# The end of an attention + soft-MoE kernel: PSUM bank order, filler matmuls, and a second queue for stores

**Chip, cores and metric.** One core of one Trainium2 chip. The metric is the device time of one execution in microseconds (us). Times from a trace are counted from the start of its span.

## The reference

The attention takes q, k, v of 8 x 12 x 448 x 64 in f32, with a soft cap on the scores. Its output, 3584 rows of 768, goes through a soft mixture of experts with 32 slots.

```python
def _attn_ref(q, k, v, cap):
    scores = scale * np.matmul(q, k.transpose(0, 1, 3, 2))
    scores = cap * np.tanh(scores / cap)
    ... softmax over the keys ...
    return np.matmul(attn, v)

def _moe_ref(x, phi, w1, w2):          # x: 3584 x 768, 8 experts, 4 slots each, F = 1024
    logits = x @ phi
    d = softmax(logits, axis=0)        # dispatch: over the rows
    slot_input = (d.T @ x)             # 32 x 768
    slot_out = relu(slot_input[e] @ w1[e]) @ w2[e]     # for each expert e
    c = softmax(logits, axis=1)        # combine: over the slots
    return c @ slot_out                # 3584 x 768, f32: 11 MB to store
```

The result is 11.0 MB. A softmax over all rows stands between the attention and the experts, so no row can be stored before the last row of attention is done.

## The kernel before

The kernel is scheduled by hand: the order of calls is the order of instructions on each engine. A tile framework adds the waits. It gives out the banks of PSUM (the memory into which TensorE writes) and the semaphores (counters) on which the completion of a DMA is counted. There are three places to know.

The attention's end. The pools of scores (`sc`, two tiles of three banks) and of `pv` (one bank) are closed, and a pool of seven banks takes their place. Its tiles `pvm` and `pvl` hold the last two pairs of heads, and `junk` is the target of filler matmuls. A filler is a 128x128 matmul of ones whose result nobody reads.

```python
    exp_part(NCH - 1, 0, CL)
    exp_part(NCH - 1, CL, CH)
    attp.close()
    big = mid.enter_context(tc.tile_pool(name="big", bufs=7, space=PSUM, reuse_waits="tile"))
    ...
    pvm = [bank([P, 2, VW], name=f"pvm{half}") for half in range(2)]
    junk = bank([P, P], name="junk")
    pv2 = [bank([P, 2, VW], name=f"pvl{half}") for half in range(2)]
    x_transp(last - 2)
    for half in range(2):
        pv_tiles(last - 1, half, 0, NT, pvm[half])
        norm(last - 1, half)
    logits(NQ - 2, bank([P, NG, NS], name="lpl"))
    busy(6)
    ...
```

The reloads of w2. The second layer's weights that don't fit in SBUF during attention lie in DRAM as bf16 and are read back, 384 KB at a time, by SyncE's queue (SP), first the first column halves, then the second. The last of them, `w2t60` of half 1, is used by the last four matmuls of the second layer.

```python
    for half in range(2):
        for n0 in range(R2, len(blocks), 4):
            t = tl.tile([P, 4, HD], BF16, name=f"w2t{n0}_{half}")
            sp.dma_start(out=t, in_=w2d[(n0 - R2) // 4][:, half, :, :])
            w2t[n0, half] = t
```

The stores. The output goes out as 24 half tiles of 192 KB (`obh`) and then 16 whole tiles of 384 KB (`ob`). VectorE (DVE) and ScalarE (ACT) take turns in moving a tile out of PSUM. The first ten half tiles are computed between the matmuls of the second layer's second half. All stores are issued by SP.

```python
    for n0 in range(0, n2, 4):
        layer2(n0, 1)
        if n0 >= 4 and n0 % 8 == 4 and done < NH - 2:
            for eng in ("act", "dve"):
                half_tile(done, 0, bank([P, HD], name="op0"), eng)   # matmul, evict, store
                done += 1
```

The softmax here doesn't subtract the row's maximum and nothing guards it: scores larger than these inputs give would overflow.

## Time and profile before

| | kernel before |
|---|---|
| device time, median of the first 3 runs | 326.57 us (326.3 to 327.66) |
| span of the profiled run | 325.5 us (this run: 327.26) |
| last tanh ends, last norm of the attention starts | 271.63, 277.33 |
| last reload issued | 281.8 |
| first store issued | 292.42 |
| DMA engines full from | 295.4 |
| 99% of the stored bytes moved, last byte landed | 323.2, 324.0 |

ScalarE limits the first 270 us (tanh and exp). After that one short step waits for another until the stores begin. Then the DMA engines are full, and the end comes when the bytes are out. So there are two ways to gain: start the stores earlier, or move more bytes in the first us of the store stage. The prediction shows the lines of the chain and of the windows. One more view is needed, SP's own timeline (start, duration of the group, line, what, count):

```profile
279.90 2.51 SPq L565 DMA_DIRECT2D w2t<-w2d  x5
292.42 7.80 SPq L624 DMA_DIRECT2D out_dram<-obh  x13
```

Five reloads are issued by 282.4, and then nothing until the first store at 292.42: the reloads are long issued when the stores begin.

### The profile page before, as it was taken

The numbers are of one execution on the slowest core, as the hardware profiler recorded it, in microseconds if no ns is written. First come the engines' busy times: TensorE is split into PE (matmuls) and PEld (weight loads), VectorE is DVE, ScalarE is ACT, GpSimd is POOL, SyncE is SP. The second block draws the span as 40 slices with busy tenths as digits, with TensorE's granted clock in tenths as the row PEclk, the third lists the DMA queues.
The fourth block names the chain that finished last, engine by engine and source line by source line (L and its number), as shares of the span: only waits on it lengthen the run. The fifth ranks groups of instructions, "written<-read, shape, count | busy, mean of one in ns | idle before, by whom it ended". The sixth has DMA issues, their size and how long they took to land.

```text
span 325.5 us, 8742 instructions
## 1 busy us (share of the span) xinstructions
PE 275.4 (85%) x3776; PEld 193.0 (59%) x3776; DVE 168.8 (52%) x428; ACT 283.5 (87%) x205; POOL 104.6 (32%) x133
## 2 busy tenths in 40 slices
PE   7889998889889988998889888988898877998570
PEld 6556666666666766666566666756666657642220
DVE  3535664466447653665466546644565343327442
ACT  2998999999999999999999999999999996226450
POOL 2064524533443353345334524452443020200000
PEclk9999999999999999999999999999999997999855
DMA  8689999999999989999999999999999435757997
GB/s 256 203 172 238 211 274 236 219 237 252 241 202 247 253 190 228 259 265 224 207 250 251 233 200 238 264 248 192 231 258 210 125 96 196 255 233 286 373 397 302
DMA packets 58486, 76.89 MB, mean 236 GB/s; under 512 B 3920, under 2 KB 54096, under 8 KB 58448
## 3 DMA queue, kind: packets, MB, share of 16 engines
q0 software_dynamic: 30480, 25.22, 51.1%
q1 hardware_dynamic: 27680, 50.67, 46.1%
q8 instruction: 29, 0.48, 0.6%
q10 hardware_dynamic: 288, 0.46, 0.4%
q14 instruction: 9, 0.07, 0.1%
HBM read 90.54 MB, written 18.09 MB: 334 GB/s over the span
## 4 chain that ended last, share of the span: by engine, by line
ACT 78%; PE 11%; DMA 3%; DVE 3%; issue 2%; SPq 1%; DVEq 0%; ACTq 0%
ACT ex L253 39%; ACT ex L257 38%; PE so_ps L609 2%; PE hp L583 2%; DMA out_dram<-ob 1%; PE op L635 1%; SPq L624 1%; DMA kraw<-in_k_dram 1%; PE junk L455 1%; PE sc L246 1%; PE pvm L274 1%; PE op L678 1%; DVE ob L682 1%; DMA out_dram<-obh 1%; PE pvl L274 1%
## 5 line engine op out<-in xcount | busy, mean ns | idle before, releaser
L253 ACT ACTIVATE ex<-sc 128x1344 bf16<-128x1344 f32 x112 | 161.6, 1712 | 2.7 <-PE sc L246 1.4
L257 ACT ACTIVATE ex<-ex 128x2688 bf16<-128x2688 bf16 (+2 forms) x57 | 160.2, 2831 | 0.1
L274 PEld LDWEIGHTS <-ex 128*128 128x128 bf16 x1344 | 79.6, 98 | 22.9 <-DVE xq L285 14.3
L274 PE MATMUL pv<-vbd,ex 128*128 128x130 bf16 x1288 | 90.4, 220 | 2.6 <-ACT ex L257 1.5
L246 PE MATMUL sc<-qT,kT 64*64 64x448 bf16 x672 | 78.8, 358 | 12.6 <-ACT ex L253 11.3
L224 POOL CAST vbd<-vraw 64x896 bf16<-64x896 f32 x23 | 21.4, 929 | 106.0 <-PE pv L274 81.3
L284 DVE RECIPROCAL rec<-pv 128x4 f32<-128x4 f32 x92 | 16.8, 183 | 60.1 <-PE pv L274 60.1
L246 PEld LDWEIGHTS <-kT 64*64 64x64 bf16 x672 | 28.3, 105 | 29.4 <-issue 11.7
L285 DVE TENSOR_TENSOR xq<-pv,rec 128x256 bf16<-128x256 f32 x92 | 39.1, 425 | 3.2
L455 PEld LDWEIGHTS <-ones 128*128 128x128 bf16 x446 | 27.7, 102 | 12.0 <-DVE xq L285 8.6
L328 POOL COPY e<-E 128x512 bf16<-128x512 bf16 x9 | 5.5, 610 | 88.4 <-ACT E L322 50.3
L455 PE MATMUL junk<-ones 128*128 128x128 bf16 x413 | 30.7, 221 | 3.0 <-DVE xq L285 1.9
L216 DVE COPY kT<-kps 128x896 bf16<-128x896 bf16 x23 | 14.4, 625 | 29.4 <-PE kps L214 29.4
L105 POOL DMA_DIRECT2D w1b<-in_moe_w_dram x32 | 24.9, 781 | 0.0
L225 POOL CAST vbd<-vraw 64x896 bf16<-64x896 f32 x23 | 24.0, 1042 | 1.3
L302 DVE COPY xT<-xps 128x512 bf16<-128x512 bf16 x47 | 19.5, 415 | 2.1 <-PE xps L300 2.1
L300 PE MATMUL xps<-ident,xq 128*128 128x128 bf16 x188 | 18.3, 220 | 0.7 <-DVE zacc L339 0.7
L203 DVE CAST kbf<-kraw 128x896 bf16<-128x896 f32 x22 | 17.2, 780 | 0.0
L216 DVE COPY qT<-qps 128x896 bf16<-128x896 bf16 x23 | 14.2, 618 | 4.5 <-PE qps L214 4.5
L214 PE MATMUL kps<-ident,kbf 128*128 128x128 bf16 x161 | 12.8, 219 | 4.2 <-DVE slacc L374 2.2
L214 PE MATMUL qps<-ident,qbf 128*128 128x128 bf16 x161 | 12.8, 219 | 3.2 <-DVE lg L316 2.7
L214 PEld LDWEIGHTS <-kbf 128*128 128x128 bf16 x161 | 10.0, 97 | 9.0 <-issue 8.3
(100 smaller groups left out, 232.5 us busy)
## 6 DMA issues: line engine op xcount, KB each, us to landing
w1b<-in_moe_w_dram POOLq DMA_DIRECT2D x32, 384.0 KB, 8.7
vraw<-in_v_dram SPq DMA_DIRECT2D x23, 448.0 KB, 4.6
qraw<-in_q_dram SPq DMA_DIRECT2D x22, 448.0 KB, 7.6
kraw<-in_k_dram SPq DMA_DIRECT2D x22, 448.0 KB, 5.2
w2d<-in_moe_w_dram POOLq DMA_DIRECT2D x18, 384.0 KB, 9.3
w2t<-w2d SPq DMA_DIRECT2D x18, 384.0 KB, 5.5
out_dram<-ob SPq DMA_DIRECT2D x16, 384.0 KB, 3.9
w2b<-in_moe_w_dram POOLq DMA_DIRECT2D x14, 384.0 KB, 9.0
```

Of the source, the lines that this page charges most:

```text
L105: pool.dma_start(out=w1b[e][:, js, fs], in_=w1r[:, e, js, fs])
L214: pe.transpose(ps[:, c, :], src[:, c, :], ident)
L216: dve.tensor_copy(t, ps)
L224: pool.tensor_copy(t[0:HP, :, :, 0:DH], raw[0:HP])
L225: pool.tensor_copy(t[HP:P, :, :, DH + 1:VW - 1], raw[HP:P])
L246: pe.matmul(sc[cs, u, 0:S], qkT["k", Q][r, c, cs], qkT["q", Q][r, :, cs], start=True, stop=True)
L253: act.activation(exs[j][:, half * CS:half * CS + CS, :], scores.pop(i)[:, :, 0:S], ACT.Tanh, scale=qk_scale / cap)
L257: act.activation(exs[j][:, u0:u1, :], exs[j][:, u0:u1, :], ACT.Exp, scale=cap)
L274: pe.matmul(pvs[pr, half][:, n, 0:VW], exs[j][:, u, GOFF[g]:GOFF[g] + P], vbds[Q % 2][:, h, c, :], start=(c == 0 and n == 0), stop=(c == N ...
L285: dve.tensor_tensor(xq[Q][:, 2 * half:2 * half + 2, h * P:(h + 1) * P] .rearrange("p g (i d) -> p g i d", i=2), pv[:, :, :, 0:DH], rec.to_ ...
L302: dve.tensor_copy(t, ps)
L455: pe.matmul(junk if home is None else home, ones, ones, start=True, stop=True)
```

## The change

The intent is threefold. One: ask for the banks at the attention's end in the order in which they come free, so that `pvm` need not wait for the last tanh. Two: add fillers in the last two steps, so that TensorE keeps its full clock. Three: issue the stores of ScalarE's tiles on ScalarE's own DMA queue, so that SP need not order all of them.

```diff
+    for j, slot, n in ((NCH - 2, "c", 6), (NCH - 2, "d", 10), (NCH - 1, "a", 8), (NCH - 1, "d", 10)):
+        at(j, slot, spare, n)
...
+    pv2 = [bank([P, 2, VW], name=f"pvl{half}") for half in range(2)]
+    lp2 = bank([P, NG, NS], name="lpl")
     pvm = [bank([P, 2, VW], name=f"pvm{half}") for half in range(2)]
     junk = bank([P, P], name="junk")
-    pv2 = [bank([P, 2, VW], name=f"pvl{half}") for half in range(2)]
...
-    logits(NQ - 2, bank([P, NG, NS], name="lpl"))
-    busy(6)
+    logits(NQ - 2, lp2)
+    busy(10)
...
-    def store(n, h0, h1, src):
+    def store(n, h0, h1, src, eng):
-        sp.dma_start(out=bass.AP(tensor=out.tensor,
+        eng.dma_start(out=bass.AP(tensor=out.tensor,
...
-        store(n, half, half + 1, ob)
+        store(n, half, half + 1, ob, act if eng == "act" else sp)
...
-        store(n, 0, 2, obs[n].rearrange("p a d -> p (a d)"))
+        store(n, 0, 2, obs[n].rearrange("p a d -> p (a d)"), sp if n % 2 else act)
```

## The prediction

> **What bounds the kernel now.** I read the page first (shares, slices, chain), then the chain of waits in order of time, then windows over the end. For the first 270 us ScalarE is the limit: the page's slices give ACT 9 tenths nearly throughout, and the chain spends 78% of the span in tanh and exp. None of the three parts touches that work, so the question is only what stands after the last tanh, at 271.6 us of a 325.5 us span. The chain of waits there (start, duration, what):
>
> ```profile
> 269.26 2.37 ACT ex L253 x2
> 271.63 0.05 issue
> 271.68 2.27 PE pvm L274 x28
> 273.95 0.21 PE lpl L311 x8
> 274.16 0.64 PE junk L455 x6
> 274.80 0.43 PE xps L300 x4
> 275.23 1.66 PE pvl L274 x20
> 276.89 0.17 PE junk L455 x3
> 277.06 0.24 PE pvl L274 x4
> ```
>
> The pair of pvm starts when the last tanh ends, although its data (the exp of the step before) is older: the wait is for the PSUM bank. Then TensorE is the chain until the last norm starts at 277.33, and slowly. Windows of one clock period each (the columns that matter: PE busy in us, then, after POOL, granted clock, DMA share, GB/s):
>
> ```profile
> 269.38:272.79 3.41, 1.52 (x26) 1.32 (x24) 1.18 (x5) 3.38 (x3) 0.00 (x0) 1.00 0.73 234
> 272.79:276.20 3.41, 3.41 (x41) 3.41 (x39) 1.74 (x6) 1.41 (x2) 0.00 (x0) 0.50 0.35 137
> ```
>
> PE was busy 1.52 of 3.41 us, and in the next 3.41 us it got half its clock. From 277.3 to 291 the chain is short DVE and ACT steps, then both expert layers on TensorE. The end is something else:
>
> ```profile
> 293.20:295.40 2.20, 2.20 (x30) 0.61 (x30) 1.49 (x3) 1.33 (x4) 0.00 (x0) 1.00 0.30 105
> 295.40:301.00 5.60, 4.59 (x39) 1.75 (x39) 4.60 (x8) 3.63 (x7) 0.00 (x0) 1.00 1.00 367
> 301.00:306.60 5.60, 3.86 (x31) 2.04 (x30) 3.15 (x5) 2.47 (x4) 0.61 (x1) 1.00 1.01 365
> 306.60:311.00 4.40, 1.97 (x6) 0.70 (x6) 1.46 (x3) 1.80 (x2) 0.00 (x0) 0.54 1.02 393
> ...
> 316.00:323.50 7.50, 1.24 (x4) 0.17 (x2) 1.94 (x2) 1.37 (x2) 0.00 (x0) 0.50 1.00 396
> ```
>
> From 295.4 to 323.5 the DMA engines are busy 1.00 at 366 GB/s (half tiles, 1536-byte rows) and then 395 GB/s (whole tiles). All stores are issued by SP; the first was issued at 292.42, the second took SP 1.94 us to issue (292.85 to 294.79; the others 0.40), and so little moved before 295.4. Evictions are ahead of the stores: the last ends at 319.0, the last transfer at 323.5. So the end is set by bytes: 24 x 192 KB and 16 x 384 KB, 4.72 MB at 0.366 and 6.29 MB at 0.395 MB/us, 12.9 + 15.9 = 28.8 us, plus 1.5 us lost near the front (323.5 - 293.2 - 28.8), plus 2.0 us of closing waits in the span. The runs' median is 1.07 us above the span (326.57 - 325.5), which I carry over.
>
> **What the Trainium skill says.** "TensorE: Matmul & The Clock Gate", Part 1 on the clock gate: the array starts and falls back to half clock, a free-running window of about 3.4 us decides. The trace agrees: 1.00, then 0.50 for 3.41 us, then 1.00. It adds that 44% busy in a window was not enough here. "DMA: Bandwidth & Descriptors", "Issuing engines are not separate DMA queues": transfers of all issuing engines share the 16 DMA engines, and a second issuer saves only issue time. The trace agrees: in 3.0 to 3.5 us SP's and ACT's queues load together at 405 GB/s, in 5.5 to 6.0 SP's alone at 405. Same page, "Anatomy of one DMA": a wait for a semaphore is made by the issuing sequencer before dispatch. In this trace SP's issue of the last reloads stood waiting 6.8 us on PE.
>
> **Part one, the banks.** In order, pvm now gets banks of the tanh before the last, free about 270.4 (two tanh of 1.19 end at 271.63). It could start 1.2 us earlier. But it cannot start before what now stands ahead of it.
>
> **Part two, the fillers.** 34 matmuls of 128x128, 0.056 us each at full clock (8 of them at 280.67 took 0.61 with 0.16 of tail), 1.9 us. Each group uses the pv bank, so it waits for the norm of the pass before, and the next pass waits for it. Following the trace's times: the group of 6 waits for the norm that ends 265.8, the last scores move from 265.06 to 266.2 (they are needed at 270.4, slack). Logits and 10 fillers end about 267.7; pv of pair 45 first half then runs 267.7 to 268.5 (before, 267.6, it was waiting for exp). Its norm ends 269.2; 8 fillers to 269.7; second half to 270.5; norm to 271.2; 10 fillers to 271.8; transposes to 272.1. So pvm starts at about 272.2, half a microsecond later than now: the fillers eat what the bank gives. They buy the clock: busy goes above 80% in 269 to 272, so 28 matmuls at 0.058 (14 of them at 264.16 took 0.98 with tail) need 1.62 instead of 2.27, then logits 0.2 and 10 fillers 0.56 cover the norm, transposes 0.23, 20 pvl 1.16, fillers 0.17, 4 pvl 0.23. Sum 4.2 against 5.65 (277.33 - 271.68). Net: 272.2 + 4.2 = 276.4, against 277.3. Gain 0.9 us (0.2 to 1.7) for everything after.
>
> **Part three, the stores.** 12 half-tile and 8 whole-tile stores go to ACT's queue. Cost there: 0.40 us of issue after each 0.58 us eviction; ACT is not the bound. Gain: SP no longer orders all stores. But the built program shows a side effect. Eight completion semaphores are dealt out in turn over both queues, and a transfer waits for the previous user of its semaphore. The last reload (w2t60, half 1) is now dealt the semaphore of ACT's second store, and SP stands in order behind it. Before, it was issued at 281.8. Times: ACT's first eviction ends 292.39 - 0.9 = 291.5, store issued 291.5 to 291.9; second eviction 291.95 to 292.53, issued 292.57, lands 2.0 later (the shortest landing of these stores) at 294.6; reload issued then, lands 3.1 later (shortest of the reloads) at 297.7. The second layer's last four matmuls need it, at 296.3 - 0.9 = 295.4 otherwise. So PE waits about 2.3 us, and all of SP's (VectorE's) stores start at 295, not 292. Meanwhile ACT alone feeds the queue, one 192 KB store per 1.0 us: 3 stores, 0.59 MB, have moved by 295.4 (before: about 0.23 MB). From then on there is enough: seven ready half tiles and the reload. Left at 295.4: 4.72 - 0.59 = 4.13 MB at 0.366 (11.3), 0.39 MB reload (1.0), 6.29 MB (15.9): 28.2 us, end 323.6, against 323.5. If SP's 1.94 us stall is gone and the first landing is quick, up to 1 us better; central end 323.1.
>
> So 0.9 us from the attention's end and about 1 us from the parallel start are given back by one misplaced reload in the store stage (1.0 us of bytes) and ACT alone feeding it. Central: 326.57 - 0.4 = 326.1.
>
> **Rivals.** (a) The intended story: the attention's end gives its full 1.2 + 1.4 us and stores start at once and saturate; first bytes at 293.2 - 2.6 = 290.6, last at 319.4, with closing waits and the 1.07 a time of about 322.5. For it: the front idle is visible. Against: the fillers' waits and the reload's semaphore. (b) Two queues raise the rate: at 5% over 28 us, 1.4 us less, about 325. Against: 405 GB/s both ways at the start. (c) The waits starve the stores: PE's stall leaves about 0.8 MB of evicted backlog (2 us of DMA) when it resumes; then ACT needs 0.58 + 0.40 + waits, about 1.05 us per pair of half tiles, 375 GB/s, barely over 366. If the reload takes the 5.5 us median, the stall is 4.7 us, the backlog runs dry, and the time is about 328. (d) ACT blocked in issue holds evictions late: whole tiles took SP 0.9 us each to issue; 0.9 + 0.9 per two tiles is still under the 2.0 us they need.
>
> **Range and chances.** Part two's spread (-0.8 to +0.7), the reload (+1.5), the queue's rate (-1) and the runs' own scatter (326.3 to 327.66) give 324.5 to 327.9. 2% is 6.5 us; everything removable at the end is under 5, and no rival costs that much: within 2% is nearly certain.
>
> **What would show it.** Right: clock 1.00 from 269 to 279; pvm starting at or after 271.7, its 28 matmuls under 1.8 us; the last reload issued after 293 and landing near 297; PE waiting over 1.5 us there for it; SP's first store after 294; DMA share 1.00 from about 295.4 to the end, at the same 366 and 395 GB/s. Wrong: the reload issued near 281 (my reading of the semaphores fails; then about 324.5), a higher rate in the saturated windows, gaps in the DMA share after 297, or the half clock still there.

## The result

| | before | after |
|---|---|---|
| device time, median of 4 runs | 326.44 us (324.86 to 327.66) | 330.11 us (329.85 to 331.12) |
| span of the profiled run | 325.5 | 328.3 |
| pvm starts, last norm starts | 271.68, 277.33 | 272.72, 277.09 |
| last reload issued | 281.8 | 295.13 |
| second layer's last matmul starts | 296.18 | 298.98 |
| first store issued | 292.42 | 292.18 |
| 99% of the stored bytes moved, last byte landed | 323.2, 324.0 | 325.2, 326.8 |

The ratio is 1.0121, with a 95% interval of 1.0072 to 1.017. A ratio here is the mean time of one kernel's fast runs over the mean of the other's fast runs of the same rounds, so it is not quite the ratio of the medians that I quote. Executions over 1.5% slower than the fastest of the same kernel are left out of the means. The kernel is 1.2% slower. That is "within 2%", but the time lies 2.2 us above the top of my range (327.9).

The chain of waits of the changed kernel (start, duration, what), at the attention's end and at its last link in this view:

```profile
272.66 0.22 PE xps L300 x4
272.89 1.60 PE pvm L274 x28
274.49 0.19 PE lpl L311 x8
274.68 0.57 PE junk L457 x10
275.25 0.26 PE xps L300 x4
275.51 1.15 PE pvl L274 x20
276.66 0.17 PE junk L457 x3
276.83 0.24 PE pvl L274 x4
...
296.21 4.50 DMA out_dram<-obh
```

The 28 matmuls of pvm take 1.60 instead of 2.27 us, so the full clock was kept. But they begin a whole us later, and the last norm gains only 0.24 us. The last line is new: ScalarE's fifth store needs 4.50 us to land, and the chain runs through it: in the built program ScalarE's sixth store has the same semaphore, and it is issued at 300.79, just after the fifth has landed (300.71). In the kernel before, the chain in this stretch is TensorE, VectorE and ScalarE work, with no DMA in it.

SP's timeline of the changed kernel:

```profile
279.67 15.78 SPq L569 DMA_DIRECT2D w2t<-w2d  x5
295.54 6.69 SPq L628 DMA_DIRECT2D out_dram<-obh  x8
```

The same five reloads now span 15.78 us instead of 2.51. The last of them is issued at 295.13, and SP's first store, which stands behind it, at 295.54. The views of what each engine waited for (total us, times, longest) say why, for SP in 290 to 302, and what that did to TensorE in 291 to 300. SP stood 9.5 us until a store had landed:

```profile
SPq L569 <- DMA out_dram<-obh: 9.5, 1, 9.5
PE so_ps L613 <- DMA w2t<-w2d: 2.9, 1, 2.9
```

And the windows of the store stage (after POOL: granted clock, DMA share, GB/s):

```profile
293.00:296.00 3.00, 3.00 (x44) 1.05 (x43) 2.08 (x4) 1.73 (x4) 0.00 (x0) 1.00 0.54 197
296.00:297.00 1.00, 0.10 (x4) 0.00 (x0) 0.00 (x0) 0.18 (x1) 0.00 (x0) 1.00 1.03 80
297.00:298.00 1.00, 0.00 (x0) 0.00 (x0) 0.00 (x0) 0.00 (x0) 0.00 (x0) 1.00 0.69 267
298.00:303.00 5.00, 3.20 (x12) 1.00 (x12) 2.85 (x5) 1.74 (x3) 0.00 (x0) 0.67 1.04 384
```

Up to 296 the engines are half busy, because ScalarE alone feeds them. From 296 to 297 they are "busy" (1.03) but move only 80 GB/s: in the packet records the first ten packets of the late reload take 0.3 to 1.3 us each (most later ones 0.12), and ScalarE's store of 295.20 begins to move only at 297.6. From 296 to 298 TensorE does next to nothing. Saturation comes at 298, not at 295.4.

The front in numbers: from 293 to 298 the kernel after moved 3 x 197 + 80 + 267 = 938 KB, of which part belongs to the reload. The windows of the prediction give the kernel before 2.2 x 105 + 2.6 x 367 = 1,185 KB in 293.2 to 298, all of it stores. The rates after 298 are those of before (366 to 397 GB/s), but there are 0.39 MB more to move. One us is an exception: from 309 to 310 the share is 0.76, at 285 GB/s. No store was issued between 307.07 and 308.62, so the engines ran short of stores once more, at a cost of some 0.3 us.

### The profile page after: what moved, and what is told of

Same layout as the page of the kernel before. It is cut to its first block, busy times and chain, and to the rows that moved or that the text cites.

```text
span 328.3 us, 8804 instructions
## 1 busy us (share of the span) xinstructions
PE 276.7 (84%) x3814; PEld 194.3 (59%) x3814; DVE 168.7 (51%) x428; ACT 283.7 (86%) x205; POOL 104.4 (32%) x133
## 4 chain that ended last, share of the span: by engine, by line
ACT 75%; PE 14%; DVE 3%; DMA 3%; issue 2%; ACTq 0%
ACT ex L253 37%; ACT ex L257 36%; DMA out_dram<-ob 2%; PE junk L457 2%; PE hp L587 2%; PE op L682 2%; PE pv L274 1%; DMA out_dram<-obh 1%; PE sc L246 1%; PE boot L457 1%; PE so_ps L613 1%; ACT obh L643 1%; PE op L639 1%; DVE xq L285 1%; DVE obh L641 1%
## 5 line engine op out<-in xcount | busy, mean ns | idle before, releaser
L274 PEld LDWEIGHTS <-ex 128*128 128x128 bf16 x1344 | 78.8, 97 | 20.6 <-DVE xq L285 13.6
L457 PEld LDWEIGHTS <-ones 128*128 128x128 bf16 x484 | 29.7, 101 | 14.3 <-DVE xq L285 11.0
L457 PE MATMUL junk<-ones 128*128 128x128 bf16 x451 | 33.2, 219 | 4.9 <-DVE xq L285 3.1
```

The lines of the kernel that those rows point to most:

```text
L274: pe.matmul(pvs[pr, half][:, n, 0:VW], exs[j][:, u, GOFF[g]:GOFF[g] + P], vbds[Q % 2][:, h, c, :], start=(c == 0 and n == 0), stop=(c == N ...
L457: pe.matmul(junk if home is None else home, ones, ones, start=True, stop=True)
```

## The experiments

The theory after reading the trace (A): the late reload, and SP's stores standing behind it, are the whole loss; parts one and two do nothing. Rivals: the fillers or the banks hurt; ScalarE loses time as an issuer; two queues move less than one. TensorE's gap, in what follows, is the longest time from the start of one matmul of the second layer to the start of the next; it is 3.19 us in the change.

All kernels gave correct results. Medians in us, with the runs of before on the same chip and rounds:

| run | what | median | before | ratio (95%) |
|---|---|---|---|---|
| e1_stores_only | part three alone | 330.67 | 326.19 | 1.0115 (1.0091 to 1.0139) |
| e2_banks_fillers | parts one and two alone | 326.21 | 326.19 | 1.0005 (0.9985 to 1.0025) |
| e3_reload_on_act | change, last reload by ScalarE | 330.41 | 326.19 | 1.0134 (1.0108 to 1.016) |
| e4_banks_only | part one alone | 326.10 | 326.19 | 0.9989 (0.9963 to 1.0015) |
| e5_reload_on_pool | change, six reloads by GpSimd | 326.37 | 325.83 | 1.0061 (0.9984 to 1.0138) |
| e6_late_stores | change, ScalarE's queue from the 11th store | 327.25 | 325.83 | 1.0056 (1.0033 to 1.008) |
| e7_banks_late_act | part one, ScalarE's queue later still | 325.95 | 325.83 | 1.0012 (0.9981 to 1.0044) |
| e8_plus38_elsewhere | before, 38 fillers in mid-attention | 326.11 | 325.83 | 1.0021 (0.9992 to 1.0049) |
| e9_late_reload_one_queue | before, last reload issued late | 328.27 | 326.36 | 1.0047 (0.9997 to 1.0097) |
| e10_pvm_in_early_bank | before, pvm in a bank that is free earlier | 324.75 | 326.36 | 0.992 (0.9862 to 0.9978) |
| e11_early_bank_late_act | e10 with ScalarE's queue late | 324.09 | 326.36 | 0.9912 (0.9873 to 0.995) |
| e12_reload_ok_sp_held | e5, SP's stores held back | 327.81 | 325.70 | 1.008 (1.0047 to 1.0114) |

The medians are over all runs of a kernel, the ratios over its fast ones. In an occasional execution of any kernel (before: 330.56 in the rounds of e5; e5: 330.83; e1: 334.11) everything is some 4 us later. In the traces of e1 and e5 this delay is already there in the first 20 us. It has nothing to do with the change, but e5's interval is wide because of it, and the trace of e5 is shifted by 4 us.

**e1, part three alone.** Edit: the three store hunks of the diff and nothing else.

> The kernel before with the third part alone (stores of ScalarE-evicted tiles on ScalarE's queue). Theory A (the last reload, w2t60 half 1, is dealt the completion semaphore of ScalarE's second store and SP stands in order behind it): that reload is issued near 295.5 instead of 281.8, TensorE waits over 2 us for it before the second layer's last four matmuls, and the time is 2.5 to 4 us above before, so 329 to 330.5: the whole loss of the change is in this part. Rival B (the loss is in the fillers, 76 more PE instructions and their waits): within 1 us of before.

Measured: 330.67 us. The reload is the last thing SP issues before its stores, as in the change (at 300.1, in a trace shifted by 4 us), and TensorE's gap is 3.85 us. The whole loss is in part three.

**e2, parts one and two.** Edit: the other hunks.

> Parts one and two without part three: all stores on SP. Theory A: the reload is issued near 281.5 again, no TensorE wait for it; the last norm starts 0.2 us earlier than before (277.1), so 326.0 to 326.6, unless an instruction fetch of PE (16 KB on one DMA engine, about 1 us) falls into the store stage, which adds up to 1.2 us at the very end. Rival B: 329 or more.

Measured: 326.21 us against 326.19. The reload is on time, the clock is kept, pvm's 28 matmuls take 1.61 us, and the time is that of before. The gain of the clock and the time spent in the fillers cancel: counted from the end of the last exp, the last norm starts 3.04 us later, against 3.13 in before.

**e3, the last reload on ScalarE's queue.**

```diff
-            sp.dma_start(out=t, in_=w2d[(n0 - R2) // 4][:, half, :, :])
+            (act if half and n0 >= 60 else sp).dma_start(out=t, in_=w2d[(n0 - R2) // 4][:, half, :, :])
```

> The changed kernel with one edit: the last reload (w2t60 half 1) is issued by ScalarE, ahead of its own stores, so no reload stands behind a store; the stores stay on two queues. Theory A: the reload is issued near 278 to 283, no TensorE wait, DMA saturated from about 294; 325 to 327, 3 to 5 us under the changed kernel. Rival C (two store queues, or ScalarE blocked by its own issues, cost by themselves): still 328.5 or more.

Measured: 330.41 us, but it doesn't test what it should. The eight semaphores are dealt out over both queues, so another reload of SP met one of ScalarE's, and SP's last three reloads slid to 289.5, 291.5 and 292.5. TensorE's gap shrank to 1.42 us, yet SP's first store came at 298.2, and ScalarE was held too:

```profile
ACT obh L642 <- DMA out_dram<-obh: 3.7, 1, 3.7
```

Moving one transfer to the other queue only moved the crossing to other transfers. A clean test needs an issuer with semaphores of its own, which is e5.

**e4, part one alone.** Edit: the order of the bank calls, `busy(6)` left.

> Part one alone. If the bank was the wait, the first pvm matmul starts near 270.5 (before: 271.68) and, with the clock dropping as before, the last norm starts 0.5 to 1.2 us earlier than 277.33; time 325.3 to 326.2. If pvm is then held by something else (transposes, exp), it starts after 271.4 and the time is that of before.

Measured: 326.10 us, and in TensorE's timeline pvm still waits for the last tanh:

```profile
271.37 2.88 PE L274 MATMUL pvm<-vbd,ex 128*128 128x130 bf16 x28 [1.17 <-ACT ex L253]
```

The brackets give the idle time before the group and what ended it: 1.17 us, ended by ScalarE, as in the kernel before. The built programs say why: in before, in this kernel and in the changed kernel the banks are the same, pvm0 in bank 1 and pvm1 in 7, junk in 2, pvl in 5 and 3, lpl in 6. The last scores lie in banks 1 to 3, and those before them in 4 to 6. The order of the calls did not decide the bank. Part one changed nothing.

**e5, the reload in time with both queues.** Edit on the change:

```diff
-            sp.dma_start(out=t, in_=w2d[(n0 - R2) // 4][:, half, :, :])
+            (pool if half and n0 >= 40 else sp).dma_start(out=t, in_=w2d[(n0 - R2) // 4][:, half, :, :])
```

> The changed kernel with the last five reloads (w2t40 to w2t60, half 1) issued by GpSimd, whose transfers have semaphores of their own; the stores stay on two queues. In the first attempt (the last reload on ScalarE) the lateness only moved to other reloads; here none stands behind a store in the built program. Theory A: every reload is issued before 284, TensorE does not wait for one, SP's first store comes at about 292.5, and the time is 324.5 to 326.5. Rival C (two store queues cost by themselves): no late reload, yet 328.5 or more.

(The edit moves six reloads, not five: w2t40, 44, 48, 52, 56 and 60.)

Measured: 326.37 us, three of the four runs between 326.02 and 326.55. The fourth, 330.83, takes the interval up to 1.0138; the three lie 3.3 us or more under every run of the change. TensorE's longest gap in the second layer is 1.00 us, as in before. With the trace shifted by 4 us, the first three us of the stores read

```profile
297.00:300.00 3.00, 3.00 (x46) 1.13 (x46) 2.18 (x4) 1.72 (x4) 0.00 (x0) 1.00 0.96 346
```

against 0.54 and 197 GB/s in the change. The late reload, with what stood behind it, is the loss. And two store queues from the start, with everything in time, gain nothing over e2.

**e6, ScalarE's queue only from the 11th store.** Edit on the change: `act if eng == "act" and n + 100 * half >= 10 else sp`.

> The changed kernel with the first ten half-tile stores back on SP; ScalarE's queue is used from the eleventh on, after all reloads. Theory A: the reload is issued near 282 again, no wait on TensorE: 325 to 327. Rival C: the 15 remaining stores on ScalarE's queue still cost, 328 or more.

Measured: 327.25 us; the reload is issued at 281.6 and TensorE's gap is 1.00 us. It removes most of the loss, but there is a dip where the second queue takes over:

```profile
299.00:301.00 2.00, 0.97 (x4) 0.38 (x4) 1.17 (x3) 1.14 (x3) 0.00 (x0) 1.00 0.62 227
```

Two us at 227 instead of 366 GB/s are 0.28 MB, or 0.8 us. SP waited there for a store to land (window 296 to 300):

```profile
SPq L627 <- DMA out_dram<-obh: 2.4, 1, 2.4
```

In the built program SP's next store has the semaphore of ScalarE's first, which landed at 299.39; SP issued at 299.45. So the dip is a crossing of the same kind, between two stores.

**e7, no fillers, ScalarE's queue for the second-half and whole tiles.** Edit on e4: the store hunks with `act if eng == "act" and half else sp`.

> Part one, no fillers, and ScalarE's queue only for half 1 of the half tiles and for the whole tiles. Theory A: as banks alone, 325 to 326.2, at best 0.5 lower because the tail has no instruction fetch in it; the candidate for a version that beats both. Rival C: 328 or more.

Measured: 325.95 us, the same as before. There is no dip, and the second queue is worth nothing.

**e8, the fillers' instructions elsewhere.** Edit on before: four groups of spare matmuls (8, 10, 10, 10) in steps 23, 30, 37 and 44.

> The kernel before with 38 more filler matmuls (76 PE instructions, as many as the change adds) in the middle of attention, nothing else. If the PE instruction fetch is what lengthens the tail: one more 16 KB fetch than before (30), one of them inside the store stage (after 300 us), the time from 99% of the stored bytes to the last byte 1.2 us or more instead of 0.6 to 0.8, and 0.3 to 1.0 us over before. If not: the same tail and the same time as before.

Measured: 326.11 us, not told apart from before. The trace is the instructive part. TensorE's instructions are read in 16 KB packets, 29 in the trace of before for 7,552 instructions. In the kernel before one such packet is under way at 293.0, when SP issues its second store, and that issue takes 1.94 us. Here it is over by 292, and SP issues seven stores where it had issued three. Before, and then e8, over 292 to 295.3:

```profile
292.42 2.84 SPq L624 DMA_DIRECT2D out_dram<-obh  x3
```

```profile
292.26 3.30 SPq L626 DMA_DIRECT2D out_dram<-obh  x7
```

But another packet now falls into the saturated stage (308.6, 948 ns), and the time from 99% of the bytes to the last one grows from 0.8 to 1.6 us. What the front gains, the tail gives back in part.

**e9, a late reload with a single queue.** Edit on before: the last reload is left out of the loop and issued by SP after the fourth store.

```diff
-            sp.dma_start(out=t, in_=w2d[(n0 - R2) // 4][:, half, :, :])
+            if (n0, half) != (len(blocks) - 4, 1):
+                sp.dma_start(out=t, in_=w2d[(n0 - R2) // 4][:, half, :, :])
...
+                if done == 4:
+                    n1 = len(blocks) - 4
+                    sp.dma_start(out=w2t[n1, 1], in_=w2d[(n1 - R2) // 4][:, 1, :, :])
```

> Kernel before with one move: the last reload (w2t60, half 1) is issued by SP after the fourth store; every store stays on SP, so nothing crosses between queues. It isolates the lateness of the reload. Theory L (the lateness alone, whatever the queues): reload issued near 295, PE idle over 2 us before its last four second-layer matmuls, DMA share under 0.8 somewhere in 295 to 298, and 329 to 330.5 us, as in the change. Theory M (the lateness costs only its own bytes in the saturated stage, 0.39 MB at 0.366 MB/us or 1.1 us, and the rest of the 3.7 us comes from SP's stores having stood behind it with only ScalarE feeding): the same PE gap, but stores five to ten keep the engines busy meanwhile, and 326.9 to 328 us. I give M 0.6.

Measured: 328.27 us, 1.9 above before. This is near theory M's band and outside theory L's, though the interval of the ratio just includes 1. TensorE's gap, 3.78 us, is longer than in the change, so the gap alone does not make the whole loss. The windows:

```profile
293.00:295.00 2.00, 2.00 (x32) 0.77 (x31) 1.24 (x2) 1.16 (x2) 0.00 (x0) 1.00 0.57 202
295.00:296.00 1.00, 0.00 (x1) 0.00 (x0) 0.00 (x0) 0.00 (x0) 0.00 (x0) 1.00 1.06 232
296.00:297.00 1.00, 0.00 (x0) 0.00 (x0) 0.00 (x0) 0.00 (x0) 0.00 (x0) 1.00 0.62 172
297.00:298.00 1.00, 0.00 (x0) 0.00 (x0) 0.00 (x0) 0.00 (x0) 0.00 (x0) 0.54 0.98 376
```

Again there is a us with full engines and a low rate when the reload starts (232 GB/s at 1.06). By the medians lateness alone costs 1.9 us. Its bytes are 1.1 us of that (0.39 MB at 0.366 MB/us). The other 0.8 fits the two us from 295 to 297, in which 0.40 MB moved where 0.73 would have at that rate.

The trace of e9 shows something else, which its edit has no part in. The end of attention is that of before, and pvm has the same wait of 1.17 us for the last tanh. But the clock stayed at 1.00, so pvm's matmuls were fast and the last norm started 1.87 us after the end of the last exp, not 3.13:

```profile
271.62 1.78 PE L274 MATMUL pvm<-vbd,ex 128*128 128x130 bf16 x28 [1.17 <-ACT ex L253]
269.77:273.19 3.42, 1.95 (x32) 1.78 (x32) 1.19 (x5) 3.39 (x3) 0.00 (x0) 1.00 0.76 270
```

These windows are the clock's own, counted back in steps of 3.413 us from its next change in the trace. Here they cut the idle time before pvm in two: TensorE is busy 57% of this window and of the one before it, where before had one of 45%. Of the six traces with the old end of attention and no fillers there, five have the half clock (before, e1, e4, e7, e8) and this one does not. So the half clock costs 1.26 us, and not in every execution. This weakens the 1.9 us. Of the other three runs of e9 only the mean clock over the whole run is on record. If all four had the full clock here and the runs of before the half, lateness would cost up to 3.2 us, near what theory L has. From the first store's issue to the last byte, which the clock of the attention does not touch, it is 33.72 us here, 31.58 in before and 30.5 to 30.9 in e4, e7 and e10: 2.1 to 3.2 us. So e9 shows that lateness costs without a second queue, but does not settle between M and L.

**e10, pvm in a bank that is really free earlier.** Edit on before: two pools, of three and four banks, instead of one of seven, and a list that deals the tiles out.

```diff
-    big = mid.enter_context(tc.tile_pool(name="big", bufs=7, space=PSUM, reuse_waits="tile"))
+    big_b = mid.enter_context(tc.tile_pool(name="big_b", bufs=3, space=PSUM, reuse_waits="tile"))
+    big_c = mid.enter_context(tc.tile_pool(name="big_c", bufs=4, space=PSUM, reuse_waits="tile"))
+    turns = iter("ccbbbcccbbccbcbbb" + "ccccb" * 8)
...
-        return big.tile(shape, dt, name=name, tag="b")
+        pool_ = {"b": big_b, "c": big_c}[next(turns)]
+        return pool_.tile(shape, dt, name=name, tag="k")
```

> Kernel before with the seven banks cut into a pool of three (the banks of the last scores) and one of four (the others), and the tiles dealt by hand: in the built program pvm0 now really lies in a bank of the scores before the last, and waits for ScalarE's instruction 174 instead of 175. No fillers, no second queue. If the bank is the wait: pvm starts about 1.1 us earlier (first matmul about 3.6 us before the last exp ends, against 2.51), the last norm 0.8 to 1.5 us earlier, first store as much, and 325.0 to 325.6 us. Rival: the exp parts or the half clock take the wait's place and the last norm moves under 0.4 us, 325.8 to 326.6.

Measured: 324.75 us, ratio 0.992, faster than before. The four fast runs have a mean of 324.3. TensorE's timeline and the windows:

```profile
270.05 0.38 PE L300 MATMUL xps<-ident,xq 128*128 128x128 bf16 x4 [0.72 <-DVE zacc L339]
270.42 1.78 PE L274 MATMUL pvm<-vbd,ex 128*128 128x130 bf16 x28
```

```profile
269.40:272.80 3.40, 2.75 (x48) 2.46 (x47) 2.12 (x9) 3.37 (x3) 0.00 (x0) 1.00 0.77 230
272.80:276.20 3.40, 3.00 (x44) 2.45 (x43) 1.82 (x7) 1.53 (x3) 0.00 (x0) 1.00 0.34 132
```

Two of the six runs (328.86 and 332.28) count as slow and are left out of the ratio; their cause was not looked for. pvm follows the transposes without a wait. Counted from the end of the last exp, it starts 3.70 us before it instead of 2.51, and the last norm starts 0.85 us after it instead of 3.13. That is a gain of 2.28 us, more than I expected. The bank is 1.0 of it: e9's trace has its clock windows at the same place, keeps the full clock too, and has the last norm at 1.87. The other 1.26 is the clock, which stays at 1.00 without a single added filler. That the earlier start does this shows in e11 and e7, whose clock windows also lie alike: in the window that ends near the start of e7's pvm TensorE is busy 2.62 of 3.42 us in e11, and the clock is kept (last norm at 0.86); it is busy 1.52 of 3.41 in e7, and the clock halves. This is the gain that parts one and two of the change were after.

**e11, the same with ScalarE's queue late.** Edit on e10: the store hunks as in e7.

> The kernel of e10 with ScalarE's queue used as well, but only for its second-half and whole tiles, so that no reload is dealt a semaphore of a ScalarE store. If two queues are worth nothing in the saturated stage, the same as e10 within 0.3 us; if there is anything in them, up to 1 us faster than e10. This is the candidate for a version that beats both kernels: 324.5 to 325.6.

Measured: 324.09 us, all six runs between 323.73 and 324.33. Against e10's fast runs (mean 324.3) this is no difference. It is the steadiest version that beats both kernels: 2.3 us under before (medians of the same rounds), and 6.0 under after's median, which is from other rounds.

**e12, the reload in time and SP's stores held back.** Edit on e5: SP issues one tiny load into a spot that ScalarE's second store reads, so it waits until that store has landed, and the store of tile 1 comes behind it.

```diff
+        if (n, half) != (1, 0):
+            store(n, half, half + 1, ob, act if eng == "act" else sp)
...
+                if done == 2:
+                    sp.dma_start(out=obs[0, 0][0:1, 2, :],
+                                 in_=bass.AP(tensor=q.tensor, offset=0, ap=[[HD, 1], [1, HD]]))
+                    store(1, 0, 1, obs[0, 0][:, 1, :], sp)
```

> The kernel of e5 (the whole change, the last five second-half reloads issued in time by GpSimd) with one thing added: before its first store SP issues one tiny load that must wait until ScalarE's second store has landed, so that all of SP's stores stand back until about 295, as they do behind the late reload, while the reload itself is in time and TensorE does not wait. If the held SP queue is what the late reload cost beyond its own lateness (e9: 1.9 us of 3.7), this is 1.5 to 2.2 us slower than e5's 326.4: 327.9 to 328.6, with the DMA share under 0.6 up to about 296. Rival: the lost time needs the slow reload in the queue itself (its first packets took 0.3 to 1.3 us each); then SP held only shifts the start and this is within 0.7 us of e5: 326.0 to 327.1.

Measured: 327.81 us, 0.1 under the expected band and well above the rival's. SP's first store is issued at 295.20, and the windows are

```profile
293.00:295.00 2.00, 2.00 (x29) 0.66 (x32) 1.38 (x3) 1.16 (x2) 0.00 (x0) 1.00 0.53 196
295.00:296.00 1.00, 1.00 (x25) 0.47 (x18) 0.52 (x2) 0.58 (x1) 0.00 (x0) 1.00 0.55 195
296.00:297.00 1.00, 0.76 (x4) 0.21 (x3) 1.00 (x3) 0.58 (x1) 0.00 (x0) 1.00 1.01 369
```

Up to 296 they are the change's windows (0.54, 197). But at 296 the engines go at once to 369 GB/s, where the change had 80.

## Why the prediction was wrong

The direction of the mechanism was right. The last reload did get the semaphore of ScalarE's second store, SP did stand behind it, and TensorE did wait. Its price was sized too low, and the gain at the attention's end too high.

**Banks.** "pvm now gets banks of the tanh before the last" failed: the bank stayed bank 1 (e4 and the built programs). It did no harm to the number, since I had the fillers delay pvm anyway. It hid the real chance, which e10 shows.

**Fillers.** That the clock would be kept was right: 28 matmuls took 1.60 against my 1.62, and from the start of pvm at 272.89 in the chain to the norm at 277.09 it is 4.2, as summed. The start was wrong: 272.7 instead of 272.2. The chain shows the two groups of fillers ahead of pvm with a tail of their own (8 in 0.64, 10 in 0.71), where I had counted 0.056 us for each filler. So the gain was 0.24 instead of 0.9 us. I had also taken the half clock of before for a fixed cost; e9's trace shows an execution without it.

**The reload.** The issue was 295.13 against 294.6 predicted, and TensorE waited 2.9 against 2.3. These sizes are near. (Its 0.39 MB at 0.366 MB/us are 1.1 us, not 1.0.)

**The step that failed** is "From then on there is enough: seven ready half tiles and the reload", with the DMA full from 295.4. In the trace it is full from 298. By then my numbers had 0.59 MB plus 2.6 us at 0.366, or 1.54 MB; 0.94 MB had moved. The missing 0.60 MB is 1.65 us at 0.366 MB/us. Of this, 0.22 MB was missing before 296, when ScalarE alone fed the engines (197 GB/s), and 0.39 from 296 to 298. I had counted an issued transfer as moving at once at the full rate, but the reload's first packets are slow, and the store beside them stood still meanwhile (80 GB/s at a share of 1.03; e9 shows the like with one queue, and e12 has none of it without a reload).

**The SP stall.** I took the central value 0.5 us below my sum for a front without SP's 1.94 us stall. The stall did go, but SP was idle there instead, waiting.

**The tail.** I did not foresee 0.8 us. From 99% of the bytes to the last it is 1.6 us after and 0.8 before. Every trace with one of TensorE's instruction packets inside the saturated stage has 1.2 to 1.7 (after, e2, e3, e5, e6, e8, e12), and every trace without one 0.5 to 0.8 (before, e1, e4, e7, e9, e10, e11). The change's 38 extra matmuls shift these packets. That the packet is the cause is likely, but no run removes the packet alone.

**The base.** I carried 1.07 us from the span to the runs' median, but the profiled run of before was 0.7 slower than that median. Both profiled runs lie 1.76 above their spans, so 0.7 us of the miss is in the starting point.

The sum: 1.65 + 0.5 + 0.8 + 0.7 = 3.65 of the 4.0 us between 326.1 and 330.1. The rest, 0.35, is about the 0.3 us of the dip at 309, and it is inside the scatter too.

The experiments do not divide the 3.7 us cleanly. The lateness of the reload alone costs 1.9 us by the medians, and 2.1 to 3.2 by the store stage of the traces (e9). SP's stores held back, with the reload in time, cost 1.6 us by the medians (e12 is 2.1 over its before, and e5, which it was made from, 0.5), and 1.4 by the store stage (32.46 against 31.10). Both cost, then, but they need not add up, and the parts come from different chips with a scatter of about 0.5 us each. What each has in the change is not shown.

**The rivals.** (c), starved stores, was the nearest, with 328. It had them starve after 298, when the backlog had run dry; in fact they starved mainly before that, because SP's ready stores stood behind the reload. Its dry backlog did come, for about 1 us at 309, but cost only some 0.3 us. (b) was refuted: the saturated rates are the same with one queue and two, and e5, e7 and e11 gain nothing from the second. (a) failed at both ends: its attention gain was never there, because the bank didn't change, and its early saturation was undone by the reload.

**Left open:** whether SP's stall and the tail are caused by the instruction packets, or only come with them; and whether e11 with those packets shifted away from the stores' start would gain another us. In its trace SP's second store still took 2.11 us to issue.

## What to carry to other kernels

When stores move to a second queue, look up in the built program which completion semaphore every neighbouring load now shares, and with whom: one load of 384 KB that ended up waiting for a store of the other queue cost more than a second queue could ever give in a stage limited by bytes. Check that a reordering of buffers changes the addresses before counting on it. And when a clock drops for want of work, first remove the wait that leaves the engine idle: that won 2.3 us where added fillers won nothing. Look at more than one trace before counting on such a drop: of six with the same work at that place, one did not have it.

## What the Trainium skill lacked or had wrong

- "TensorE: Matmul & The Clock Gate", Part 1: it names busy and idle windows of about 3.4 us, but not what share of a window counts as busy. Here 1.52 of 3.41 us busy (45%) was followed by half the clock, and in e9 1.95 of 3.42 (57%) by the full clock.
- "Runtime: NRT & Kernel Launch", Instruction fetch mechanics: it says that fetching blocks of 16 KB is mostly hidden. Here such a packet took 0.9 to 1.6 us near and in the store stage. In six traces (before, e4, e7, e9, e10, e11) one came while SP issued its first stores, and one issue of SP took 1.2 to 2.1 us there instead of 0.4; in three (e2, e6, e8) it came earlier, and every issue took about 0.4. Packets inside the saturated stage go with tails of 1.2 to 1.7 us instead of 0.5 to 0.8.
- "DMA: Bandwidth & Descriptors", Issuing engines are not separate DMA queues: its statement that a second issuer saves only issue time holds (366 and about 395 GB/s with one queue and with two). It lacks that the completion semaphores, here eight dealt over both queues, can tie a transfer of one queue to a store of the other: the reload was issued at 295.13 instead of 281.8, and the kernel took 3.7 us more.
- No page that I found says that the start of a DRAM read shows as busy DMA engines that move little: first packets of 0.3 to 1.3 us each, and a us at 80 GB/s with a DMA share of 1.03. Stores are not needed for it: in before, the reload issued at 277.59 with no store about has first packets of 0.2 to 0.6 us.
